# A third buffer for V, V's loads at other places, and a later opening behind each projection

## The chip, the cores and the metric

The kernel runs on one core of one Trainium2 chip. Its time is the device time of one execution in microseconds (us); the time of a version is the median of its runs. Five engines work side by side, each in the order of its own queue: TensorE (PE in the profile; its weight loads are PEld), VectorE (DVE), ScalarE (ACT), GpSimd (POOL) and SyncE (SP), which here only issues DMAs. Engines wait for each other, and for DMAs, through semaphores.

## The reference

Attention over normalised queries and keys, and behind it a feed-forward layer with x * cos(x):

```python
batch, n_heads, seq, head_dim = (8, 12, 448, 64)     # d_model 768, d_ff 2048, 3584 tokens
q_n = q / (norm(q) + 1e-06);  k_n = k / (norm(k) + 1e-06)
scores = q_n @ k_n.T / tau                            # tau = 0.1
attn = exp(scores - max(scores));  attn = attn / (sum(attn) + 1e-09)
x = (attn @ v) as [3584, 768]
h = x @ w_in;  g = h * cos(h);  out = g @ w_out
```

Inputs and output are float32. The kernel computes with bfloat16 operands and float32 sums.

## The kernel before

**Tiling.** The 96 heads are taken as 48 pairs of heads (g = 0 to 47). Three pairs make a unit (u = g // 3, 16 of them), two units a batch (6 pairs, 8 batches). Loads are made by unit, attention by pair, and the feed-forward layer by batch: the projection by w_in (`m1`) for all 448 tokens of a batch, the product with w_out (`m2`) in tiles of 128 tokens.

**A unit's way in.** SyncE loads the unit's k and q (`load`, raw). GpSimd squares them (sq, line 558), VectorE reduces the squares (n, line 565), ScalarE makes the reciprocal root by Ln and Exp (lnn and rn, lines 579 and 582), GpSimd multiplies (qks, line 590, labelled scale3.2 for unit 3, pair 2). A DMA transpose from SyncE's queue (line 607) puts the result into qkT; the first nine pairs are transposed on TensorE instead. V is loaded by `load_v` on GpSimd's DMA queue, two DMAs of 192 KB for a unit, into one of two buffers va (u % 2), so that the loads of a unit wait until the unit two before it has been used up.

**A pair.** `pair(g, f)` writes the scores of pair g (`scores(g, c)`, c = 0 to 3, on TensorE into the banks SC1, SC0, SC1, SC0, each followed by an Exp on ScalarE, line 652), and between them the product attn @ V of pair g - 1 (`attend`) and pieces of the output product (`m2_fill`, the four numbers in f, counted in steps of 0.16 us). `attend` has three stages. Stages 0 and 1 (R, line 669) open the accumulation of the values (with V) and of the sums of the exponentials (with ones) in the bank AV; they need one seventh of the keys (`exp` of c = 0). Stage 2 (lines 676 to 700) adds the rest.

**The way out of a pair.** For the pairs in `direct` (0 to 5 and 9 to 11), ScalarE makes the reciprocal of the sums by Ln and Exp (lines 728 and 730), and xT is made at once (line 736). For all others the unnormalised values and the sums are copied to xu (line 723), and once a unit `chain(u)` runs: four small DMAs on SyncE's queue gather the unit's sums (`gather`, line 745), VectorE adds and inverts them (rcp, lines 750 and 753), one DMA writes them to DRAM (`spread`, line 754), two bring them back spread over partitions (`bcast` into RB, line 756), and GpSimd multiplies (xT, line 760; labelled x17 for pair 17).

**Projections.** `m1(b)` is eight groups of 12 matmuls of 448 columns, over three bank pairs (AV, SC0, SC1). Behind each group ScalarE makes the cosine by Sin (line 789) and VectorE the product gT (line 791), which frees the bank. `m1` of batch 0 runs before pair 6, those of batches 1 to 6 behind the pairs 13, 21, 27, 33, 39 and 45 (`points`), with some steps of the output product behind them, and that of batch 7 at the end. The last group of a projection in `points` goes to AV, the one before it to SC1. ScalarE changes its table between Exp and Sin.

**Who sets the order.** TensorE's order is the order of the program, except in the prologue, where a window of 24 operations is open (and where matmuls on zeros fill its idle time). On the other four engines the order is made by a planner (`arrange` and `play`): it plays the program with costs, gives every operation a due time (`late`), and takes the ready one that is due first. DMAs are played as a flow with a time to take off (TAKEOFF), a time to land (LANDING), a share (`weight`) and a duration (`bulk`, the number behind the semaphore's name in each `dma` call); a transpose has an additional `lead`. `behind` (found by `find(label)`) puts an operation behind the issue of another one on the same engine. What comes out is a fixed queue for each engine.

## Time and profile before

| | |
|---|---|
| median of 3 runs | 442.57 us (442.4 to 443.27) |
| the profiled execution | 442.96 us |
| its span, first to last instruction | 441.2 us |
| granted TensorE clock | 0.998 |
| ScalarE, GpSimd, VectorE busy | 270.0, 227.9, 188.6 us |
| bytes moved by DMA | 64.80 MB, mean 147 GB/s |
| V: 32 DMAs of 192 KB, issue to landing, median | 8.8 us |
| k and q: 96 DMAs of 224 KB, median | 6.4 and 7.3 us |
| gathers of sums: 52 DMAs of 5.2 KB, median | 2.8 us |
| transposes: 39 DMAs, median | 4.5 us |

The page and the answers of the trace are read so. A row of a timeline has the start in us from the span's start, the time, the engine and line, the operation, and output<-input; in square brackets stands how long the engine was idle before it and what ended the wait. A row of the waits names who waited for whom, then the sum in us, the number of times and the longest. An idle engine costs nothing unless something that sets the end waits for it.

### The profile page before, as it was taken

Reading aid. Unit: us, or ns where it says so; the run is one execution under the profiler, and the core shown is the slowest. Engines: PE = TensorE matmul, PEld = TensorE weight load, DVE = VectorE, ACT = ScalarE, POOL = GpSimd, SP = SyncE. Lnnn points to the kernel's source line nnn. Section 1 sums busy time; section 2 is a strip of 40 time slices with the busy share of each in tenths; the row PEclk is TensorE's granted clock in tenths of the full one; section 3 lists DMA queues with packets and bytes.
Section 4 is the critical chain, followed back from the end, with each engine's and each line's share of the span. In section 5 each row is a group of like instructions: output and inputs, shape, how many; then the busy total and the mean of one; then the engine's idle time right before and its main releaser. Section 6 shows DMA issues by size and latency. Waiting matters only on the chain.

```text
span 441.2 us, 13512 instructions
## 1 busy us (share of the span) xinstructions
PE 419.4 (95%) x6049; PEld 231.2 (52%) x6049; DVE 188.6 (43%) x243; ACT 270.0 (61%) x352; POOL 227.9 (52%) x182
## 2 busy tenths in 40 slices
PE   7899979979998999999999999999999999999996
PEld 3344536635554645565556655565556645555563
DVE  3552852445833248330952158221952134223421
ACT  5886568685586755876487745786478745703400
POOL 4998909577390295916756095908656043002000
PEclk9999999999999999999999999999999999999999
DMA  8999999999358999649943997969966960151022
GB/s 193 248 252 218 250 184 144 180 193 201 78 85 141 173 206 198 114 109 212 242 106 74 175 218 157 129 133 217 213 100 90 140 139 3 39 138 36 1 71 71
DMA packets 80713, 64.80 MB, mean 147 GB/s; under 512 B 45712, under 2 KB 75408, under 8 KB 80656
## 3 DMA queue, kind: packets, MB, share of 16 engines
q1 hardware_dynamic: 62528, 51.16, 58.3%
q0 software_dynamic: 18048, 12.59, 19.0%
q8 instruction: 47, 0.77, 0.8%
q10 hardware_dynamic: 80, 0.20, 0.1%
q14 instruction: 10, 0.08, 0.1%
HBM read 56.13 MB, written 11.15 MB: 153 GB/s over the span
## 4 chain that ended last, share of the span: by engine, by line
PE 68%; DMA 10%; ACT 7%; issue 5%; POOL 4%; DVE 3%; SPq 2%; ACTq 0%; DVEq 0%; POOLq 0%
PE SC L774 18%; PE AV L774 10%; PE TP L849 9%; PE PO L849 8%; PE AV L676 5%; PE SC L637 5%; DMA sums<-xu 4%; ACT PX L652 3%; DMA va<-in_v_dram 2%; PE PO L879 2%; POOL xT L760 2%; PE AV L669 2%; POOL qks L590 2%; PE SC L879 2%; PE TP L879 2%
## 5 line engine op out<-in xcount | busy, mean ns | idle before, releaser
L652 ACT ACTIVATE PX<-SC 128x448 bf16<-128x448 f32 (+1 forms) x192 | 153.5, 824 | 33.7 <-PE SC L637 20.9
L849 PE MATMUL TP<-W,gT 64*64 64x384 bf16 x1408 | 143.7, 324 | 0.4
L849 PE MATMUL PO<-W,gT 64*64 64x384 bf16 x1408 | 143.7, 324 | 0.0
L590 POOL TENSOR_TENSOR qks<-raw,rn 128x896 bf16<-128x896 f32 (+1 forms) x48 | 79.2, 1675 | 45.3 <-ACT rn L582 43.5
L774 PE MATMUL SC<-xT,W 128*128 128x448 bf16 x480 | 98.6, 353 | 1.7 <-ACT PX L652 0.9
L760 POOL TENSOR_TENSOR xT<-xu,RB 128x448 bf16<-128x448 f32 x39 | 43.2, 1136 | 109.3 <-DMA RB<-scr 109.3
L849 PEld LDWEIGHTS PO<-W,gT 64*64 64x64 bf16 x1408 | 76.2, 107 | 17.7 <-DVE osb L822 3.0
L789 ACT ACTIVATE cosb<-SC,cst 128x896 f32<-128x896 f32 x40 | 40.2, 1007 | 72.8 <-PE SC L774 69.0
L849 PEld LDWEIGHTS TP<-W,gT 64*64 64x64 bf16 x1408 | 76.2, 107 | 16.2 <-PE TP L849 2.7
L558 POOL TENSOR_TENSOR sq<-raw 128x896 bf16<-128x896 f32 x45 | 74.9, 1683 | 8.3 <-DMA raw<-in_q_dram 5.0
L774 PEld LDWEIGHTS SC<-xT,W 128*128 128x128 bf16 x480 | 45.9, 98 | 47.0 <-POOL xT L760 2.9
L791 DVE TENSOR_TENSOR gT<-SC,cosb 128x896 bf16<-128x896 f32 x40 | 43.4, 1087 | 47.5 <-ACT cosb L789 47.3
L774 PE MATMUL AV<-xT,W 128*128 128x448 bf16 x288 | 61.8, 352 | 0.1
L565 DVE TENSOR_REDUCE n<-sq 128x14 f32<-128x896 bf16 (+2 forms) x49 | 51.4, 1054 | 10.0 <-ACT sq L556 6.0
L637 PE MATMUL SC<-qkT 64*64 64x448 bf16 x576 | 52.1, 359 | 3.4 <-ACT PX L652 3.0
L723 DVE COPY xu<-AV 128x896 f32<-128x896 f32 x25 | 27.1, 1085 | 46.4 <-PE AV L692 46.4
L822 DVE COPY osb<-PO 128x384 f32<-128x384 f32 x26 | 14.5, 557 | 71.5 <-PE PO L849 65.0
L774 PEld LDWEIGHTS AV<-xT,W 128*128 128x128 bf16 x288 | 28.1, 98 | 26.6 <-issue 0.5
L789 ACT ACTIVATE cosb<-AV,cst 128x896 f32<-128x896 f32 x24 | 24.1, 1005 | 21.3 <-PE AV L774 21.3
L676 PE MATMUL AV<-PX,va 128*32 128x448 bf16 x576 | 36.2, 356 | 0.0
L669 PE MATMUL AV<-PX,va 64*64 64x224 bf16 x192 | 25.6, 259 | 5.7 <-DVE gT L791 1.9
L791 DVE TENSOR_TENSOR gT<-AV,cosb 128x896 bf16<-128x896 f32 x24 | 26.1, 1087 | 9.9 <-ACT cosb L789 9.9
(60 smaller groups left out, 345.6 us busy)
## 6 DMA issues: line engine op xcount, KB each, us to landing
raw<-in_k_dram SPq DMA_DIRECT2D x48, 224.0 KB, 6.4
raw<-in_q_dram SPq DMA_DIRECT2D x48, 224.0 KB, 7.3
out_dram<-osb SPq DMA_DIRECT2D x55, 192.0 KB, 3.5
RB<-scr SPq DMA_DIRECT2D x26, 336.0 KB, 4.8
va<-in_v_dram POOLq DMA_DIRECT2D x32, 192.0 KB, 8.8
W<-in_moe_w_in_dram POOLq DMA_DIRECT2D x4, 768.0 KB, 15.1
W<-in_moe_w_out_dram POOLq DMA_DIRECT2D x4, 768.0 KB, 23.1
sums<-xu SPq DMA_DIRECT2D x52, 5.2 KB, 2.8
```

What stands on the lines that cost most here:

```text
L558: pool(lambda e, x=x, y=y: e.tensor_tensor(y, x, x, ALU.mult), src_, dst, 0.1 + n * 1.78e-3, label="sq%d.%d" % (u, p)).pad = LATE if u > 1 ...
L565: dve(lambda e, w=w: e.tensor_reduce(out=n2v[i][:, 2 * p : 2 * p + 2, w], in_=sqv[p][:, :, w, :], axis=mybir.AxisListType.X, op=ALU.add), ...
L590: f = lambda e, s0=s0, s1=s1: e.tensor_tensor(qksv[i][:, p, s0:s1].rearrange("p s h d -> p h s d"), rawv[i][:, h, s0:s1, :], bass.AP(rn[i] ...
L637: m = e.matmul(SCv[z][BP * o : BP * o + BP, a, 0:S], t[r, c - 1 + (NT3 + 1) * o, 0:BP], t[r, :, BP : 2 * BP], start=True, stop=True)
L652: act(lambda e: e.activation(PHv[j] if c == 0 else PXv[j][:, c - 1], SCv[z][:, :, 0:n], ACT.Exp, scale=1.0 / TAU), ["SC%d" % z], [("PX", j ...
L669: m = e.matmul(AVq[64 * a : 64 * a + 64, k, :, o, :], w, PHv[j][r, a, :], start=(n == 0), stop=False)
L676: t = e.matmul(AVv[o : o + 32, 0, 0:S], vav[i][:, 2 * p + a, c + 1, d : d + 32], PXv[j][:, c, a, :], start=False, stop=(c == NT3 - 1))
L760: pool(lambda e, p=p: e.tensor_tensor(xTv[b % 2][:, UP * i + p, :], xuv[:, u % 3, p, :], RBv[i][:, p, :], ALU.mult), [("RB", i, p), ("xa", ...
L774: t = e.matmul(ph[:, a, 0:S], W1v[:, c, 128 * n : 128 * n + 128], xTv[b % 2][:, c, :], start=(c == 0), stop=(c == NKC - 1))
L789: act(lambda e, ph=ph, cz=cz: e.activation(cosv[cz], ph[:, :, 0:S], ACT.Sin, bias=cst.ap()[:, 0:1], scale=1.0), names(gi) + ["cst0"], [("c ...
L791: dve(lambda e, ph=ph, cz=cz, gi=gi: e.tensor_tensor(gTv[:, 2 * gi : 2 * gi + 2, S * (b % 2) : S * (b % 2) + S], ph[:, :, 0:S], cosv[cz], ...
L849: r = e.matmul(POH[b][x : x + 64, 0:HW], gTv[k, y, col + x : col + x + 64], W2v[k, y, HW * b : HW * b + HW], start=(y == 0 and h == 0), st ...
```

## The change

It has four parts.

- **V's buffers and loads.** va has three buffers (u % 3). Inside `pair`, the load is for unit u + 2 where it was for u + 1, and starts at pair 9: V5 behind x8, V6 behind x11, V7 without `behind` but reading the sums buffer 0 (so it waits until the gather of unit 4 has landed), V8 behind x17 and so on. Ahead of that, V2 reads xT of pair 2, V3 stands behind the load W2.3, and V4, which was loaded inside pair 9, behind scale3.2.
- **The opening behind a projection.** In the pairs 14, 22, 28, 34, 40 and 46 (g - 1 in `points`), stage 0 of `attend` for the pair before is written behind `scores(g, 0)` and the first `m2_fill` instead of ahead of them. `points` moves up so that `pair` can see it.
- **The planner's numbers.** TAKEOFF, LANDING, the lead of a transpose, and the durations (and one weight) of transposes, gathers and bcasts.
- **iot.** The index tile of the prologue has no memory of its own; it lies in cosb0.

```diff
--- before.py
+++ after.py
@@ -39,8 +39,8 @@
     OVERLAP = {"ACT": 0.09, "DVE": 0.08, "POOL": 0.0, "SP": 0.0, "PE": 0.0}
     WINDOW = 24
     PATIENCE = 0.1
-    TAKEOFF = {"SP": 1.67, "ACT": 1.67, "POOL": 1.5}
-    LANDING = 0.6
+    TAKEOFF = {"SP": 1.85, "ACT": 1.85, "POOL": 1.6}
+    LANDING = 0.45
     BOTH = 1.09
     COLD = 2.7
     ROOM = 2200
@@ -410,7 +410,7 @@
     lnn = sbs("lnn", 2, [128, UH * NB], F32)
     rn = sbs("rn", 2, [128, UH * NB], F32)
     qks = sbs("qks", 2, [128, NB * UH * D], BF16)
-    va = sbs("va", 2, [128, UH * VS * D], BF16)
+    va = sbs("va", 3, [128, UH * VS * D], BF16)
     qkT = sbs("qkT", NT, [128, 2 * S], BF16)
     PX = sbs("PX", 2, [128, NB * S], BF16)
     xu = sb("xu", [128, 5 * UP * S], F32)
@@ -422,7 +422,7 @@
     ident = sb("ident", [128, 128], BF16)
     zt = sb("zt", [128, S], BF16)
     ones = sb("ones", [128, 96], BF16)
-    iot = sb("iot", [128, 128], I32)
+    iot = cosb[0].bitcast(I32).ap()[:, 0:128]
     cst = sb("cst", [128, 2], F32)
 
     SC = [ps("SC%d" % i, [128, 2 * 512], F32) for i in range(2)]
@@ -469,7 +469,7 @@
             if label.startswith(y):
                 took, descs = ISSUE[y]
         o = P.op(eng, lambda e: [f(e) for f in fns], reads, writes, cost=took * len(fns), dma=sem, bulk=bulk, label=label)
-        o.nd, o.descs, o.lead = len(fns), descs * len(fns), 0.75 if label[0] == "T" else 0.0
+        o.nd, o.descs, o.lead = len(fns), descs * len(fns), 0.3 if label[0] == "T" else 0.0
         o.weight, o.pad = weight, pad
         if behind is not None:
             P.order_only(behind, o)
@@ -502,8 +502,8 @@
     EXPSET = "natural_log_exp_and_others"
     SINSET = "trig_and_small"
 
-    pool(lambda e: e.iota(iot.ap(), [[1, 128]], base=0, channel_multiplier=-1), (), ["iot"], 0.25)
-    dve(lambda e: e.tensor_scalar(ident.ap(), iot.ap(), 0, None, ALU.is_equal), ["iot"], ["ident"], 128)
+    pool(lambda e: e.iota(iot, [[1, 128]], base=0, channel_multiplier=-1), (), [("cos", 0)], 0.25)
+    dve(lambda e: e.tensor_scalar(ident.ap(), iot, 0, None, ALU.is_equal), [("cos", 0)], ["ident"], 128)
     dve(lambda e: e.memset(cst.ap()[:, 0:1], math.pi / 2.0), (), ["cst0"], 1)
     dve(lambda e: e.memset(cst.ap()[:, 1:2], 1e-12), (), ["cst1"], 1)
     pool(lambda e: e.memset(ones.ap()[:, 0:64], 1.0), (), ["ones"], 0.15)
@@ -527,7 +527,9 @@
                 pad=LATE if u > 1 else 0.0)
 
     def load_v(u, behind=None, reads=()):
-        i = u % 2
+        if u >= NU:
+            return
+        i = u % 3
         b, hb = u // 2, UH * (u % 2)
         dma("POOL", [lambda e, z=z: e.dma_start(
             vav[i][BP * z : BP * z + BP, :, 1 - z : NT3 + 2 - z, :].rearrange("p h x d -> p h (x d)"),
@@ -606,7 +608,7 @@
         if g >= TD:
             dma("SP", [lambda e: e.dma_start_transpose(
                 qkTv[j], qks[i].ap()[:, NB * 2 * D * p : NB * 2 * D * (p + 1)])], [("qks", i, p, 0), ("qks", i, p, 1)],
-                [("qkT", j, 0), ("qkT", j, 1)], "T%d" % j, 1.17, "T%d" % g, None, 10.0)
+                [("qkT", j, 0), ("qkT", j, 1)], "T%d" % j, 1.4, "T%d" % g, None, 10.0)
             return
 
         def half(e, bank, s0, s1):
@@ -656,7 +658,7 @@
 
     def attend(g, direct, stages=(0, 1, 2)):
         u, p, j = g // UP, g % UP, g % 2
-        i, b = u % 2, g // PB
+        i, y, b = u % 2, u % 3, g // PB
         AVq = AVv[:, :, 0:S].rearrange("p x (s o m) -> p x s o m", s=NB, o=2)
         ws = slice(0, 64) if direct else slice(32, 96)
 
@@ -665,7 +667,7 @@
                 o = n ^ k
                 r = slice(BP * o, BP * o + BP)
                 for a in range(2):
-                    w = vav[i][r, 2 * p + a, 0 if o else VS - 1, :] if k == 0 else ones.ap()[r, ws]
+                    w = vav[y][r, 2 * p + a, 0 if o else VS - 1, :] if k == 0 else ones.ap()[r, ws]
                     m = e.matmul(AVq[64 * a : 64 * a + 64, k, :, o, :], w, PHv[j][r, a, :],
                                  start=(n == 0), stop=False)
             return m
@@ -673,7 +675,7 @@
         def av(e, c):
             for o in range(0, 128, 32):
                 a, d = o // 64, o % 64
-                t = e.matmul(AVv[o : o + 32, 0, 0:S], vav[i][:, 2 * p + a, c + 1, d : d + 32], PXv[j][:, c, a, :],
+                t = e.matmul(AVv[o : o + 32, 0, 0:S], vav[y][:, 2 * p + a, c + 1, d : d + 32], PXv[j][:, c, a, :],
                              start=False, stop=(c == NT3 - 1))
             return t
 
@@ -701,7 +703,7 @@
 
         for n in stages:
             if n < 2:
-                o = P.op("PE", lambda e, n=n: rest(e, n), [("va", i), ("PX", j, 0), "ones", "zeros"], ["AVa", "AVs"],
+                o = P.op("PE", lambda e, n=n: rest(e, n), [("va", y), ("PX", j, 0), "ones", "zeros"], ["AVa", "AVs"],
                          cost=HALF, mode="Q", label="R%d" % g)
                 if n:
                     P.settled(opened[g], o)
@@ -709,7 +711,7 @@
         if 2 not in stages:
             return
         for c in range(NT3):
-            P.op("PE", lambda e, c=c: av(e, c), [("va", i), ("PX", j, c + 1)], ["AVa"], cost=MM + (0.021 if c == 0 else 0),
+            P.op("PE", lambda e, c=c: av(e, c), [("va", y), ("PX", j, c + 1)], ["AVa"], cost=MM + (0.021 if c == 0 else 0),
                  mode="C32", label="AV%d" % g)
         if not direct:
             P.op("PE", sm, ["ones", ("PX", j, 1), ("PX", j, 2)], ["AVs"], cost=MM, mode="C32", label="S%d" % g)
@@ -745,7 +747,7 @@
         dma("SP", [lambda e, r=r, a=a: e.dma_start(
             sums[i].ap()[64 * a : 64 * a + 64, SPR * r : SPR * r + SPR],
             bass.AP(xu, ((64 * a + 32 * r) * 5 + 3 + i) * UP * S, [[5 * UP * S, 1], [SPR, 64], [1, SPR]]))
-            for r in range(2) for a in range(2)], [("xs", i, p) for p in range(UP)], [("sums", i)], "sums%d" % i, 0.4,
+            for r in range(2) for a in range(2)], [("xs", i, p) for p in range(UP)], [("sums", i)], "sums%d" % i, 0.7,
             "gather%d" % u)
         dve(lambda e: e.tensor_reduce(out=rcp[i].ap(), in_=sums[i].ap().rearrange("p (r x) -> p x r", r=2),
                                       axis=mybir.AxisListType.X, op=ALU.add), [("sums", i)], [("rcp", i)], 2 * SPR,
@@ -755,7 +757,7 @@
             [("rcp", i)], [("scr", u)], "scr", 0.02, "spread%d" % u)
         dma("SP", [lambda e, a=a: e.dma_start(
             RBv[i][64 * a : 64 * a + 64], bass.AP(scr, (u * 2 + a) * UP * S, [[0, 64], [1, UP * S]])) for a in range(2)],
-            [("scr", u)], [("RB", i, p) for p in range(UP)], "RB%d" % i, 3.2, "bcast%d" % u, None, 1.0, 0.5)
+            [("scr", u)], [("RB", i, p) for p in range(UP)], "RB%d" % i, 3.4, "bcast%d" % u, None, 2.4, 0.5)
         for p in range(UP):
             pool(lambda e, p=p: e.tensor_tensor(xTv[b % 2][:, UP * i + p, :], xuv[:, u % 3, p, :], RBv[i][:, p, :], ALU.mult),
                  [("RB", i, p), ("xa", u % 3, p)], [("xT", b % 2, UP * i + p)], 1.1, label="x%d" % (UP * u + p))
@@ -947,6 +949,8 @@
         a = min(y for y in [step * x for x in range(cycle)] + [2 * NF] if y >= at) - at
         return (a + 1) // 2, a // 2, c, d
 
+    points = {PB * (b + 1) + (1 if b == 1 else 3): b for b in range(1, B - 1)}
+
     def pair(g, f):
         u, p = g // UP, g % UP
         if 3 <= u < NU - 1:
@@ -956,10 +960,12 @@
                 norms(u + 1, 1)
         late = g > PB
         quarters = g >= PB
-        if late:
+        if late and g - 1 not in points:
             attend(g - 1, direct(g - 1), (0,))
         scores(g, 0)
         m2_fill(f[0], quarters)
+        if late and g - 1 in points:
+            attend(g - 1, direct(g - 1), (0,))
         scores(g, 1)
         if late and f[1] and quarters:
             attend(g - 1, direct(g - 1), (1,))
@@ -975,8 +981,9 @@
                     chain(u - 1)
                 if g > PB and (u <= 3 or u % 2 == 0):
                     loads(u + 2, find("bcast%d" % (2 if u == 4 else u - 1)) if u > 3 else None)
-                if u + 1 < NU and u != 1:
-                    load_v(u + 1, find("x%d" % (g - 1 if u % 2 == 0 else g - 4)) if u > 4 else None)
+                if g > PB:
+                    load_v(u + 2, None if u == 5 else find("x%d" % (g - 1 if u < 5 or u % 2 == 0 else g - 4)),
+                           [("sums", 0)] if u == 5 else [])
         if g == PB:
             m2_fill(f[1], True)
         if g + 2 < PB:
@@ -1008,7 +1015,7 @@
     load_w1(3, find("scale1.0"))
     for x in range(NQ):
         load_w2(x, find("scale1.1"))
-    load_v(2)
+    load_v(2, None, [("xT", 0, 2)])
     norms(2, 0)
     norms(2, 1)
     loads(3)
@@ -1017,12 +1024,12 @@
     for g in range(PB, TD):
         transposes(g)
     m1(0, 2, NKC - 1)
-    load_v(3)
+    load_v(3, find("W2.3"))
     norms(3, 1)
+    load_v(4, find("scale3.2"))
     loads(4)
     P.free = False
     m2_add(0)
-    points = {PB * (b + 1) + (1 if b == 1 else 3): b for b in range(1, B - 1)}
     for g in range(PB, NG):
         pair(g, (0, 5, 0, 6) if g == PB else shares(3 if 2 * PB + 1 < g <= 3 * PB + 1 or g >= NG - 2 else 2))
         if g in points:
```

## The prediction

> **What bounds the kernel now.** I read the engine line of the page first, then TensorE's waits by stretch, then the timelines of VectorE, ScalarE, SyncE and GpSimd around the two stretches with the longest waits.
>
> The page says how far a gain can go:
>
> ```profile
> PE 419.4 (95%) x6049; PEld 231.2 (52%) x6049; DVE 188.6 (43%) x243; ACT 270.0 (61%) x352; POOL 227.9 (52%) x182
> ```
>
> TensorE is busy for 419.4 of the 441.2 us of the span. It works in the order written, so the end moves only by what its 21.8 us of idle time gain or lose: 5.7 in the first 44 us, 2.6 at 62 us (behind the first projection), 4.3 in the tail after its last matmul, and waits between. TensorE's waits, first from 85 to 100 us and then from 101 us to the end:
>
> ```profile
> PE SC L645 <- ACT PX L652: 1.2, 2, 0.6
> PE AV L669 <- ACT xu L728: 1.0, 1, 1.0
> PE SC L774 <- ACT PX L652: 0.9, 1, 0.9
> PE SC L637 <- ACT PX L652: 0.4, 1, 0.4
> PE AV L669 <- issue: 0.2, 1, 0.2
> ```
>
> ```profile
> PE AV L669 <- DVE gT L791: 1.9, 4, 0.5
> PE AV L669 <- DVE xu L723: 1.2, 1, 1.2
> PE SC L774 <- POOL xT L760: 0.8, 4, 0.3
> PE PO L879 <- DVE osb L822: 0.7, 1, 0.7
> ```
>
> The first list sums to 3.7 us, all of it ended by ScalarE. Why ScalarE is late stands in the timelines of SyncE, GpSimd, VectorE and ScalarE from 77 to 91 us:
>
> ```profile
> 79.11 3.33 SPq L745 DMA_DIRECT2D sums<-xu  x4
> 82.54 1.25 SPq L607 DMA_TRANSPOSE qkT<-qks  x1
> ```
>
> ```profile
> 77.97 1.35 POOL L532 DMA_DIRECT2D va<-in_v_dram  x2 [1.08 <-PE AV L692]
> ```
>
> ```profile
> 87.28 0.20 DVE L750 TENSOR_REDUCE rcp<-sums 128x21 f32<-128x42 f32 x1 [4.15 <-DMA sums<-xu]
> 87.72 2.02 DVE L565 TENSOR_REDUCE n<-sq 128x14 f32<-128x896 bf16 x2
> 89.66 0.61 DVE L735 COPY xu<-AV 128x448 f32<-128x448 f32 x1
> ```
>
> ```profile
> 89.77 0.33 ACT L579 ACTIVATE lnn<-n,cst 128x42 f32<-128x42 f32 x1 [2.87 <-DVE n L565]
> 90.28 0.53 ACT L728 ACTIVATE xu<-AV 128x448 f32<-128x448 f32 x1
> ```
>
> V of unit 4 is issued at 77.97, the gather of the sums of unit 2 right behind it at 79.11. The gather's four pieces land 5.4 to 7.5 us after issue (the reads and writes of the sums in that window). VectorE stands 4.15 us at rcp; behind it in its queue are two reductions n and the copy of pair 9; ScalarE stands 2.87 us at lnn, which wants those n, and behind lnn is the Ln of pair 9 (line 728) that frees TensorE's bank. From 90.28 ScalarE works almost without a break until 100.3, so its 2.87 us are lost to the end. The same thing happens at 126 us with V of unit 6 (issued 126.02), in VectorE's timeline:
>
> ```profile
> 135.22 0.20 DVE L750 TENSOR_REDUCE rcp<-sums 128x21 f32<-128x42 f32 x1 [4.31 <-DMA sums<-xu]
> 135.66 1.03 DVE L723 COPY xu<-AV 128x896 f32<-128x896 f32 x1
> ```
>
> Here the copy that frees TensorE's bank is behind rcp, and TensorE loses 1.2 us. A gather with no V beside it (237 to 243 us) takes this from issue to landing:
>
> ```profile
> DMA to landing us min/median/max: 2.0/2.1/2.2
> ```
>
> **(a) The gather of unit 2.** With three buffers V4 no longer waits for pair 8's matmuls (the 1.08 us before 77.97). It is free behind scale 3.2, which is the third of the six products that GpSimd runs from 65.34 in 9.92 us, so from some 70.3. By the planner's due times I put it at about 72, behind scale 4.0. Two things follow. The two squares behind V4 in the old order end 1.08 us sooner, the wait that V4 had, so one or both n can run before rcp; and the gather no longer has 384 KB starting just ahead of it. At best the 2.87 us of ScalarE's idle time go (TensorE's 3.7 are not all to be had: the bank waits behind 90.28 are ScalarE's own 10 us of work). At worst nothing: V4's bytes then precede the raw loads of 70 to 79 us, the DMA engines are as full there, and the whole queue ahead of the gather is late by as much. Between 0 and 2.87 I take 2.3: the end nearer to the undisturbed 2.1 us, but not all of it, as a transpose is issued at 82.54 right behind the gather, as one was at 130.96 in the second case.
>
> [...]
>
> **(b) The gather of unit 4.** V6 goes from 126.02 to behind x11, before the projection of batch 1, and V7 comes only after this gather has landed (it reads the sums). Without V6 ahead, the transpose issued at 127.06, which took 5.0 us to land, has 2.6 like the one issued at 123.10, and the last piece (issued 130.26, landed 135.20) has the 2.0 of one issued at 142.03, which also had a transpose 0.7 us behind it. Rcp then runs at some 132.5, the copy waits for its matmuls alone. Between 0 and 1.2 I take 1.0. V7 has GpSimd wait for the gather; queued behind it are only the products of unit 4, which wait for RB until 143.3 anyway.
>
> **(c) Opening later.** Four of the six pairs behind a projection have R (line 669) wait for the last gT: 0.46 us at 119.9, 224.6 and 323.5, 0.53 at 274.2. Now SC.0 goes first; its bank SC1 was freed one group (2.27 us) sooner. At 323.94 in TensorE's timeline R runs, then SC.0 at 324.03, three steps of the output product from 324.13 to 324.61, then SC.1. Put ahead of R, SC.0 and the three steps take 0.1 + 0.48 = 0.58 us, more than the 0.46 or 0.53. For the pairs 28, 34 and 40 the wait is gone: 0.46 + 0.53 + 0.46 = 1.45. Pair 14 has the other share (no steps between SC.0 and SC.1), so only SC.0's 0.1 moves into its wait. Pairs 22 and 46 had no wait and neither gain nor lose. Sum 1.55; if gT came later still (it is VectorE's, with n queued between), 1.0. I take 1.5.
>
> **(d) What costs nothing.** V from unit 8 on is issued at the same release as now (x17, x23 and so on), for a unit later, so with its due time later it goes behind the squares. The gathers beside projections (160 to 309 us, 6.9 to 9.2 us) may land sooner, but TensorE lost nothing to them: their results are wanted some 30 us later. If that cover were gone it would show as TensorE waiting for xT, 0.8 us in all now. V15 leaves the last projection (356.52), where nothing waits for it. The 128 columns of iot go into cosb0, first written at 46.8 us, long after ident was made of them at 1.1.
>
> **(e) The planner's new constants** change no instruction, only the order on ScalarE, VectorE, GpSimd and SyncE. TAKEOFF plus LANDING changes from 2.27 to 2.30 on SyncE and from 2.10 to 2.05 on GpSimd; a transpose is reckoned 0.2 cheaper in all, a gather 0.3 dearer. No row prices a new order. Bounds: the best is that the waits for xT and osb go too (0.8 + 0.7 = 1.5 gained), the worst that transposes come as much later (1.5 lost; the nearest of them lands 2.2 us before its scores, issued 326.37, landed 331.09, wanted 333.26). I take 0, in the middle.
>
> **The sum.** 2.3 + 1.0 + 1.5 = 4.8 us. The profiled run took 442.96 (its span 441.2 and 1.8 around it), so 438.2 for it; the median of the runs is 0.39 lower, so 437.8, with the span at 436.4. Its own range, by (a) from 1.2 to 2.87 and (e) at about half its bounds, is 436.3 to 439.3.
>
> **Rivals.**
> *The move of V4 gains nothing* because the DMA engines are full from 70 to 80 us, but (b) and (c) hold: 442.57 - 2.5 = 440.1. For it: the raw loads issued at 73.4 and 74.1 need 5.1 and 5.4 us, against 3.3 for the first load of all. Against: the n can run sooner whatever the gather does.
> *The gathers are held by the transposes*, not by V: (a) and (b) are gone, 442.57 - 1.5 = 441.1. For it: at 130 us V6 had landed at 131.1, yet the gather's last two pieces landed at 134.9 and 135.2, beside the transpose's 135.6. Against: pieces with a transpose 0.7 us behind them (142.03, 338.64) landed in 2.0 and 2.6 us.
> *Slower: V's bytes hold up the raw loads, and lnn stands at ScalarE's head.* V5 and V6 now both go out behind x8 and x11, between 96 and 101 us, where raw loads already need 5 to 7 us and GpSimd's squares wait for them (2.21, 0.34 and 0.24 us at 109 to 113). If V6 makes these loads late by its own 4.0 us (issued 126.02, first half landed 130.04), the n are late by as much, lnn, now at 120.39, blocks the exponentials of pair 14, and ScalarE's idle time costs TensorE 3.7 / 2.87 = 1.28 of itself as at 90 us: 5.1 us. V4 does the same to the squares of unit 5, and (a) is gone. 442.57 - 2.5 + 5.1 = 445.2. It decides from some 2 us of lateness on: squares end at 115, and the last n runs at 120.1 behind gT, so there are 2 to 5 us of cover, which speaks against it.
> *It does not do what it says*: the planner puts V4 and V7 beside gathers again and an order elsewhere loses what (c) gains: 442.5.
>
> **How the numbers follow.** The forecast has 0.53, V4 for nothing 0.12, transposes 0.12, slower 0.11, no effect 0.05, and 0.07 is for a gain above 6.3 (a, b and c at their best and part of (e)), below 436.3. The time is 437.8. The range goes from 435.4 (most of that last case) to 441.3, so that both partial rivals are in it and the slower one and no effect are out. A change below 0.2% (0.9 us) can't be told from none here. Faster by more: 0.53 + 0.12 + 0.12 + 0.07 = 0.84, of which 0.01 goes to the middle for a partial gain that shrinks; within it 0.06; slower 0.11.
>
> **What would show it.** For (a): V4 issued near 72, no idle time of some 3 us ahead of lnn near 90, and TensorE's waits for ScalarE from 85 to 100 at 1.5 us or less. For (b): no V between 120 and 130, rcp near 132 and no 1.2 us wait for xu. For (c): the four waits of AV L669 for gT down to one of 0.4. For (e): waits for xT and osb as they are. Wrong it is if TensorE waits for a transpose or for V, or if lnn or a product on GpSimd stands longer for raw loads than now.

## The result, and the profile after

The changed kernel is slower: 447.5 us, the median of 10 runs (443.73 to 449.01), against 441.99 us for before in the same comparison (440.73 to 443.27). The ratio is 1.0116, with a 95% interval of 1.0083 to 1.0149; a second comparison of the same two kernels (run e11 below) gave 1.0066 (1.0034 to 1.0098). Forecast were 437.8 us and a ratio of 0.989. The profiled execution took 448.73 us, its span 445.9, at a granted clock of 0.990.

The page's engine line, of after:

```profile
PE 424.0 (95%) x6054; PEld 233.2 (52%) x6054; DVE 189.2 (42%) x243; ACT 269.4 (60%) x352; POOL 227.9 (51%) x182
```

TensorE is idle for as long as before (445.9 - 424.0 = 21.9 us, before 21.8), but busy 4.6 us longer, with the same work. So waits have moved from one place to another, and the same matmuls take longer. TensorE's waits in after, from 60 to 101 us and from 101 us to the end:

```profile
PE SC L639 <- ACT PX L654: 3.0, 2, 2.6
PE TP L851 <- issue: 2.1, 1, 2.1
PE SC L647 <- ACT PX L654: 0.6, 1, 0.6
PE AV L671 <- issue: 0.2, 1, 0.2
```

```profile
PE SC L776 <- POOL xT L762: 2.9, 8, 1.1
PE SC L776 <- ACT PX L654: 1.6, 1, 1.6
PE PO L881 <- DVE osb L824: 0.7, 1, 0.7
PE AV L671 <- DVE gT L793: 0.4, 1, 0.4
PE AV L671 <- DVE xu L725: 0.3, 1, 0.3
```

What was to go has gone: of four waits of R for gT one is left, the 1.2 us for xu has become 0.3, and no wait near 90 us is for the Ln of pair 9. What has come: 2.1 us ended by "issue", which is no wait for any engine or DMA that the profile shows; and the projections' waits for xT, 2.9 us in place of 0.8. The new stall, in TensorE's timeline:

```profile
79.67 0.32 PE L851 MATMUL TP<-W,gT 64*64 64x384 bf16 x1
79.67 0.32 PE L851 MATMUL PO<-W,gT 64*64 64x384 bf16 x1
82.06 0.47 PE L851 MATMUL TP<-W,gT 64*64 64x384 bf16 x1 [2.06 <-issue]
82.06 0.52 PE L851 MATMUL PO<-W,gT 64*64 64x384 bf16 x1
```

It stands amid a run of equal matmuls of the output product, whose operands had long been there; and behind it the same matmul takes 0.52 us in place of 0.32. Busy time by stretch, of after, with the granted clock (the first number behind the five engines) and the share of the DMA engines:

```profile
64.00:68.40 4.40, 3.50 (x48) 2.21 (x52) 0.00 (x0) 3.23 (x7) 2.98 (x2) 0.61 0.32 45
79.00:82.00 3.00, 0.99 (x24) 0.36 (x13) 2.08 (x2) 1.02 (x2) 1.12 (x1) 1.00 1.25 221
82.00:85.50 3.50, 3.44 (x44) 2.47 (x47) 0.00 (x0) 0.92 (x1) 1.68 (x1) 0.51 1.09 180
```

The clock is 0.61 behind the wait of 2.6 us at 62 us, and 0.51 behind the new stall. In the trace each is a stretch of 3.41 us at half clock, which costs some 1.7 us of matmul time. In before's profiled execution the clock is 1.00 in all three stretches, though its wait at 62 us was as long.

Pairs start later or earlier than before as follows (scores of pair g, after minus before): pair 7 +1.45 (half clock), pair 10 +5.45 (stall and half clock), pair 12 +3.53 (the stall at 90 us is gone), pair 18 +2.70 (the gather of unit 4), pair 22 +4.63 (second projection), pairs 29, 35 and 41 +4.31, +4.08 and +3.57 (the openings), end +4.7.

What stood in SyncE's, GpSimd's, VectorE's and ScalarE's timelines around the first gather, in after:

```profile
72.09 1.33 SPq L609 DMA_TRANSPOSE qkT<-qks  x1
...
80.69 2.44 SPq L747 DMA_DIRECT2D sums<-xu  x4
83.96 1.23 SPq L609 DMA_TRANSPOSE qkT<-qks  x1
```

```profile
72.16 1.35 POOL L534 DMA_DIRECT2D va<-in_v_dram  x2
...
83.70 1.68 POOL L560 TENSOR_TENSOR sq<-raw 128x896 bf16<-128x896 f32 x1 [3.58 <-DMA raw<-in_q_dram]
```

```profile
89.51 0.19 DVE L752 TENSOR_REDUCE rcp<-sums 128x21 f32<-128x42 f32 x1
```

```profile
92.27 0.32 ACT L581 ACTIVATE lnn<-n,cst 128x42 f32<-128x42 f32 x1
```

V4 went out at 72.16 as reckoned, and neither rcp nor lnn has a wait in front of it. But the gather still took 5.0 to 6.1 us to land (80.69 to 87.50), the transpose issued at 72.09 took 10.0 us (that of the same pair in before 5.4), and GpSimd's square stood 3.58 us for raw loads. The DMA engines are that full: the packets that start from 70 to 79 us take 1.15 times the 16 engines' time of that stretch (1.02 in before). The trace shows one more user of them: queue q8, kind "instruction", with 47 packets and 0.77 MB in all, 16 KB each. TensorE has 6054 matmuls and as many weight loads; 0.77 MB over 12,108 is 64 bytes for each, so this is taken for TensorE's own program being fetched; that is an estimate, as the trace doesn't say for which engine the queue works. In before's first trace these blocks start at 68.10, 73.71, 79.70 and 84.07 us. In after they start at 67.57 and 77.94, and the second takes 2.46 us in place of 0.9 to 1.7.

### The profile page after: what moved, and what is told of

It is laid out like the page before. It is cut to its first block, busy times and chain, and to the rows that moved or that the text cites. A ratio compares the mean times of both kernels' runs of the same rounds, so it can differ in the third digit from the quotient of the medians.

```text
span 445.9 us, 13527 instructions
## 1 busy us (share of the span) xinstructions
PE 424.0 (95%) x6054; PEld 233.2 (52%) x6054; DVE 189.2 (42%) x243; ACT 269.4 (60%) x352; POOL 227.9 (51%) x182
## 4 chain that ended last, share of the span: by engine, by line
PE 65%; issue 9%; POOL 8%; DMA 7%; ACT 6%; DVE 2%; SPq 1%; POOLq 0%; ACTq 0%; DVEq 0%
PE SC L776 19%; PE AV L776 10%; PE TP L851 9%; PE PO L851 8%; PE AV L678 5%; PE SC L639 4%; POOL xT L762 3%; POOL qks L592 3%; ACT PX L654 3%; DMA scr<-rcp 2%; DMA RB<-scr 2%; PE AV L671 2%; PE SC L881 1%; PE TP L881 1%; PE PO L881 1%
## 5 line engine op out<-in xcount | busy, mean ns | idle before, releaser
L851 PE MATMUL TP<-W,gT 64*64 64x384 bf16 x1408 | 146.3, 328 | 2.5 <-issue 2.1
L851 PE MATMUL PO<-W,gT 64*64 64x384 bf16 x1408 | 146.1, 328 | 0.0
L851 PEld LDWEIGHTS PO<-W,gT 64*64 64x64 bf16 x1408 | 77.1, 108 | 20.8 <-issue 4.9
L851 PEld LDWEIGHTS TP<-W,gT 64*64 64x64 bf16 x1408 | 77.7, 108 | 16.5 <-PE TP L851 2.7
L639 PEld LDWEIGHTS SC<-qkT 64*64 64x64 bf16 x576 | 16.3, 106 | 23.5 <-ACT PX L654 12.5
```

Of the source, the lines that this page charges most:

```text
L639: m = e.matmul(SCv[z][BP * o : BP * o + BP, a, 0:S], t[r, c - 1 + (NT3 + 1) * o, 0:BP], t[r, :, BP : 2 * BP], start=True, stop=True)
L851: r = e.matmul(POH[b][x : x + 64, 0:HW], gTv[k, y, col + x : col + x + 64], W2v[k, y, HW * b : HW * b + HW], start=(y == 0 and h == 0), st ...
```

## The experiments

In four groups; within a group all kernels and before share a chip. Every one has five rounds against before (12 runs, e9 6).

**The parts, each alone.** e1 has only the later opening, e2 only the planner's numbers, e3 only the third buffer and V's places, and e4 is the changed kernel with V4 behind the last load of w_out (about 47 us) in place of scale3.2 (72 us):

```diff
# e4, against the changed kernel
-    load_v(4, find("scale3.2"))
+    load_v(4, find("W2.3"))
```

> The kernel before with the later opening alone. Theory (V4's bytes at 72 us hold up TensorE's instruction fetch, and the idle time halves its clock): the opening is no part of the loss; 1.0 to 1.5 us faster than before, the three gT waits of 0.5 us gone, no wait ended by issue near 80 us. Rival (the opening costs): slower than before by 1 us or more.

> The kernel before with the planner's new constants alone. Theory: within 1 us of before, no wait of TensorE ended by issue near 80 us. Rival (the planner's new order is what loses): 3 to 5 us slower.

> Third buffer and V's new places alone, with the constants and the opening of before. Theory: 4 to 6 us slower than before, as the whole change is; the transpose issued near 72 us needs about 10 us to land, TensorE waits some 2 us for issue near 80 and has half its clock in the window behind it. Rival (planner's order): within 1 us of before.

> The changed kernel with V4 right behind V3 (at some 48 us) instead of behind scale3.2 (72 us). Theory: V4 has landed by 71, the transposes of 72 and 76 us land within 6 us, the wait for issue near 80 us (2.1) and the half clock behind it (1.7 us lost) are gone: 3.8 us faster than the changed kernel, some 443.5. Rival: as slow as the changed kernel, 447.5.

Measured: e1 0.9994 (0.9966 to 1.0022), e2 0.9995 (0.9968 to 1.0021), e3 1.0084 (1.005 to 1.0118), e4 1.0034 (1.0001 to 1.0068). The loss comes with V's places: e3 alone has 0.0084, where the whole change has 0.0116 and, in e11 below, 0.0066. In e4's trace V4 lands at 66 to 68 us, the instruction blocks come at 67.22, 73.16 and 79.38, there is no stall, the transpose takes 5.1 us, and the gather of unit 2 lands in 2.0 to 2.8 us. In e1's trace the waits for gT are gone (1.66 us by the starts of the pairs), but its time doesn't show it: where 1.0 to 1.5 us were expected, the medians are 0.2 us apart, and the interval admits 1.5 us at most. e3 loses a little less than its theory's 4 to 6 us, with a stall of 0.36 us where some 2 were expected, and no half clock behind it. Both e1 and e2 leave V4 where before has it, and in their traces only 2.0 us are left of the waits that sum to 3.7 us around 90 us: the clock was halved at 65 us and the gather landed in 2.6 to 3.8 us. That wait, on which the forecast's largest term rests, is tested again with e16.

**V7, and the wait at 62 us.** e5 has V7 behind x17 in place of the gather, e6 the edits of e4 and e5, e7 is e6 with 7 matmuls on zeros written into the wait of 2.6 us, e8 the changed kernel with these. Their result is not used.

```diff
# e5, e6, e7
+                    if u == 6:
+                        load_v(7, find("x%d" % (g - 1)))
+                    if u != 5:
+                        load_v(u + 2, find("x%d" % (g - 1 if u < 5 or u % 2 == 0 else g - 4)))
-                    load_v(u + 2, None if u == 5 else find("x%d" % (g - 1 if u < 5 or u % 2 == 0 else g - 4)),
-                           [("sums", 0)] if u == 5 else [])
# e7, e8
         if g == PB:
             m2_fill(f[1], True)
+            P.op("PE", lambda e: [e.matmul(AVv[:, 0, 0:S], zt.ap()[:, 0:128], zt.ap(), start=True, stop=True)
+                                for _ in range(7)][-1], ["zt"], ["AVa", "AVs"], cost=7 * MM, mode="F", label="fill")
```

> The changed kernel with V7 behind x17 (at some 158 us) instead of behind the gather of unit 4 (136 us). Theory: V7's bytes beside the broadcast of unit 4 and the gather of unit 5 make the second projection wait 1 to 2.4 us for xT; without them that wait falls to 0.3 or less and the kernel is 2 us faster than the changed one, some 1.007 of before. Rival (V4 is all of the loss): as slow as the changed kernel, 1.011.

> V4 early (as in the run before) and V7 behind x17. Theory: both losses gone and the gains of opening later and of the free gathers of units 2 and 4 kept: 0.995 of before (2 us faster), TensorE idle for 4 us less than in the changed kernel. Rival (the gains were an accident of one trace): 1.000 to 1.003.

> The kernel with V4 early and V7 late, and seven matmuls of zeros (into the bank that is free there) in the 2.6 us for which TensorE waits behind the first projection; their result is not used. Theory (a wait of over 2 us costs another 1.7 us, since the granted clock halves for 3.4 us when the wait fills enough of a window of that length): no half clock at 65 us, 1 us faster than without them. Rival (the half clock there is made up for later, as ScalarE is behind anyway): no difference.

> The changed kernel with the same seven matmuls of zeros behind the first projection. Theory: one of its two windows of half clock goes, the one behind the wait for issue at 80 us stays: 1 to 1.7 us faster than the changed kernel, 1.008 of before. Rival (the clock is made up for later): 1.011.

Measured: e5 1.0060 (1.0025 to 1.0096), e6 1.0008 (0.9969 to 1.0046), e7 1.0003 (0.997 to 1.0036), e8 1.0056 (1.0027 to 1.0084). V7's place is not what has the second projection (the one behind pair 21) wait for xT: e5 has that wait still, 1.63 us, so its theory fails. e6 has 1.0008 where 0.995 was expected; e12 below shows part of the reason. The filled wait has no half clock behind it in the traces of e7 and e8, yet e7 is no faster than e6, and e8 is still slow: the half clock at 65 us is not the loss, or not alone. e5 to e6, V4's place alone, is 0.0052.

**V4 alone.** e9 is before with the third buffer and V4 at 72 us, every other V at its old place in the program; e10 the same with V4 at 47 us. With the third buffer, loads at their old places no longer wait for a buffer: V5 goes out at 82.6 us in e9 and 82.8 in e10 (before 94.8), V6 at 111.7 and 107.8 (before 126.0). e11 is the changed kernel once more. e12 is e6 with the planner's old numbers.

```diff
# e9 (e10: find("W2.3")), against before
+    load_v(4, find("scale3.2"))
-                if u + 1 < NU and u != 1:
+                if u + 1 < NU and u not in (1, 3):
# e12, against e6
-    TAKEOFF = {"SP": 1.85, "ACT": 1.85, "POOL": 1.6}
-    LANDING = 0.45
+    TAKEOFF = {"SP": 1.67, "ACT": 1.67, "POOL": 1.5}
+    LANDING = 0.6
...
```

> Only V of unit 4 is moved (third buffer, behind scale3.2, so about 72 us); every other load of V, the planner's numbers and the opening are those of before. Theory 'V4 at 72': its 384 KB, the raw loads and the transposes fill the DMA engines from 72 to 80 us, the block of instructions due at about 73 comes only at 77 or later, and TensorE stands 0.3 to 2.1 us near 80 us (with some half-clock time behind it): ratio 1.005 to 1.010, like the kernel with all of V moved (1.0084). Rival 'the order of spreads and transposes and V5 to V7': V4 alone costs nothing, ratio 0.998 to 1.002, or 0.995 as the prediction had it.

> The same with V4 behind the last load of w_out (about 47 us) in place of 72. Theory 'V4 at 72': the blocks of instructions come every 5 to 6 us, no stall near 80 us, the gather of unit 2 lands in 2.0 to 2.8 us, and the stall of 3.7 us at 90 us stays away: ratio 0.995 to 1.000, at least 0.006 below the kernel with V4 at 72. Rival: no difference between the two, both within 0.998 to 1.002.

> The changed kernel itself, on the same chip as the three others. Both theories: ratio 1.008 to 1.015 as in its first comparison. A trace of another execution of it: by 'V4 at 72' the block of instructions due at 73 us is again 4 us late or more, and the stall near 80 us is between 0 and 2.1 us.

> The changed kernel with V4 at 47 us, V7 behind x17, and the planner's old numbers; against the same with the new numbers (ratio 1.0008 to its before) SyncE's queue differs in the order of the spreads and the transposes: the spread of units 2, 4, 6 and 8 goes ahead of the transpose beside it again. Theory 'the order takes back what V4 and the opening gain': the spread lands within 2 us of issue, the wait for xT at the second projection falls from 0.9 to 1.6 us to 0.4 or less, and the ratio to 0.992 to 0.997. Rival 'the order doesn't matter': ratio 0.998 to 1.003, xT waits as before.

Measured: e9 1.0102 (1.0068 to 1.0136), e10 1.0035 (1.0015 to 1.0056), e11 1.0066 (1.0034 to 1.0098), e12 0.9971 (0.9944 to 0.9999). Between e9 and e10 are 0.0067, or 3.0 us, for one load's place, as the theory had it. Both are slower than they should be by something else: the planner sent V0 at 1.39 us in both, ahead of raw loads (before at 5.57), and in e10's trace pair 6 starts 3.3 us late. So e10 missed its number (0.995 to 1.000), and this pair speaks for the difference only.

e11 missed two of the three things expected of it: the ratio is below 1.008 to 1.015, and the block expected 4 us late came in time; the stall, 0.15 us, is within the 0 to 2.1 named. Its trace is another execution of the same program, with a span of 440.6 us, 5.3 us shorter, and it shows what the 5.3 us are. Waits from 60 to 101 us, then the stretches:

```profile
PE SC L639 <- ACT PX L654: 3.0, 2, 2.6
PE SC L776 <- POOL xT L762: 1.9, 1, 1.9
PE SC L647 <- ACT PX L654: 0.6, 1, 0.6
```

```profile
64.00:68.40 4.40, 3.42 (x80) 2.04 (x84) 0.00 (x0) 4.32 (x8) 2.92 (x2) 1.00 0.19 27
...
79.00:82.00 3.00, 3.00 (x83) 1.93 (x76) 1.50 (x3) 2.53 (x4) 1.02 (x1) 1.00 1.15 295
82.00:85.50 3.50, 3.35 (x78) 2.10 (x74) 2.27 (x4) 2.33 (x4) 1.68 (x1) 1.00 1.25 167
```

The wait of 1.9 us for xT, at the projection behind pair 13, is another matter and comes back under e12. Near 80 us there is no wait for issue but one of 0.15 us at 84 us, too short to show in the list, and the clock is 1.00 in all three. 2.06 for the stall and twice 1.7 for the half clock make 5.5 us; by the starts of the pairs the two executions part by 1.3 us at pair 7, by 3.9 at pair 10, and by little else. The DMA queues from 69 to 77 us, first of e11, then of after (queue, packets, MB, share of the 16 engines):

```profile
q1 hardware_dynamic: 1585, 1.17, 89.2%
q0 software_dynamic: 219, 0.11, 17.7%
q8 instruction: 1, 0.02, 1.0%
```

```profile
q1 hardware_dynamic: 1344, 1.11, 72.6%
q0 software_dynamic: 367, 0.18, 23.9%
```

In e11 a block of instructions got through at 73.53; in after none did until 77.94, beside more of V's packets (q0). V4 went out within 0.1 us of the same time in both. So with V4 at 72 us the block can come in time or late, from one execution to the next: the two traces show both. The spread of the runs shows less: the 22 of the changed kernel lie from 442.34 to 450.89 us, but the 29 of before in e11's comparison also lie as far apart as 439.16 to 445.10.

e12 came out at the edge of its theory's range (0.9971, where 0.992 to 0.997 was expected). In SyncE's queue it differs from e6 at the spreads of three units, 2, 7 and 11: with the new numbers a transpose stands ahead of each, with the old ones behind it, and two outputs move with those of 7 and 11. Around the spread of unit 2, first e6, then e12, with the first matmuls of the projection behind pair 13:

```profile
85.12 3.05 SPq L826 DMA_DIRECT2D out_dram<-osb  x2
88.21 1.34 SPq L609 DMA_TRANSPOSE qkT<-qks  x1
89.60 0.58 SPq L756 DMA_DIRECT2D scr<-rcp  x1
93.04 1.12 SPq L758 DMA_DIRECT2D RB<-scr  x2
...
101.97 1.45 PE L776 MATMUL SC<-xT,W 128*128 128x448 bf16 x4 [3.89 <-POOL xT L762]
```

```profile
84.39 2.35 SPq L826 DMA_DIRECT2D out_dram<-osb  x2
86.79 0.59 SPq L756 DMA_DIRECT2D scr<-rcp  x1
87.43 1.23 SPq L609 DMA_TRANSPOSE qkT<-qks  x1
89.20 1.12 SPq L758 DMA_DIRECT2D RB<-scr  x2
...
98.82 1.29 PE L776 MATMUL SC<-xT,W 128*128 128x448 bf16 x6 [0.94 <-POOL xT L762]
```

In e6 the spread is issued 2.81 us later, 1.38 of it for the transpose ahead and 1.43 for the output DMAs that end later, and it takes 3.42 us to land in place of 2.39. GpSimd's products of unit 2 start at 98.53 in place of 95.35, the projection stands 3.89 us for them in place of 0.94, and TensorE's clock is halved behind that, at 102.2 us: pair 14 starts 4.63 us later by it. This execution of e6 is its longest run (447.89 us). But the wait stands in six of the seven traces with the new numbers and V's new places, 1.4 to 3.9 us long (in after, the seventh, TensorE waits 1.6 us for ScalarE there), and with the old numbers and V4 moved it is 0 to 1.2 us in seven traces.

At the second projection e12 has no wait for xT over 0.2 us, while the longest in after is 1.1. There the order is not the reason: around the spread of unit 4 it is the same in all versions, a transpose 2.6 to 4.8 us ahead of the spread and the next one 0.5 to 1.2 us behind it. This spread lands in 1.6 to 1.8 us in the four traces with V6 where before has it, and in the fourteen others in 2.6 to 2.8 (e10, e12 to e15) or in 4.4 to 6.6. V7 beside it isn't needed for the late ones (e5, e6, e7 and e9 have V7 over 20 us later, and 4.4 to 5.0), nor are the new numbers (e3 and e9 have the old ones). What holds it up there stays open.

Waits of e12 from 101 us on:

```profile
PE SC L776 <- POOL xT L762: 1.3, 6, 0.5
PE PO L881 <- DVE osb L824: 0.7, 1, 0.7
PE AV L671 <- DVE gT L793: 0.4, 1, 0.4
```

**The shares.** e13 is e12 with V4 back at 72 us, e14 e12 with the opening of before, e15 e12 with the 7 matmuls on zeros of e7, e16 the kernel before.

```diff
# e13, against e12
-    load_v(4, find("W2.3"))
+    load_v(4, find("scale3.2"))
# e14, against e12
-        if late and g - 1 not in points:
+        if late:
...
-        if late and g - 1 in points:
-            attend(g - 1, direct(g - 1), (0,))
```

> The version with the planner's old numbers (V4 at 47 us, V7 behind x17, ratio 0.9971), and in it V4 alone put back to 72 us, behind scale3.2; the prologue on TensorE and its whole order are the same in both. Theory 'V4 at 72 us costs some 3 us, by the block of instructions that comes late and by TensorE's clock behind the stall': ratio 1.002 to 1.008, and single runs spread over 6 us or more. Rival 'the move of V4 is free, the loss is in the planner's new numbers': 0.995 to 0.999.

> The same version (V4 at 47 us, old numbers) with the opening of before. Theory 'the opening is worth the 1.5 us that the waits for gT in the trace say': ratio 1.000 to 1.002. Rival 'the opening gives its gain back elsewhere': 0.996 to 0.998, no different from the version with it.

> The same version with 7 matmuls on zeros in the wait of 2.6 us behind the first projection (their result is not used). Theory 'the half-clock stretches behind that wait cost 1 to 1.5 us in most executions': ratio 0.992 to 0.995. Rival 'they come as often elsewhere': 0.996 to 0.998.

> The kernel before, unchanged: a second trace of it. Theory 'the stall of 3.7 us at 90 us belongs to single executions': TensorE's waits for ScalarE from 85 to 100 us are below 2.6 us here if the clock was halved behind the wait at 62 us, and 3 us or more if not. Rival 'it is in every execution': 3.3 to 4.1 us in any case. Ratio 0.998 to 1.002 by both.

Measured: e13 1.0034 (1.001 to 1.0059), e14 0.9991 (0.9961 to 1.0022), e15 0.9985 (0.9958 to 1.0011), e16 0.9995 (0.9977 to 1.0014). V4's place by itself, with TensorE's whole order the same, is 0.0063 between e12 and e13, and the intervals don't meet (the two are of different groups). e13's profiled execution happened to be its shortest run (438.45 us). Its block came at 72.88, the next one at 81.92, and the stall is there all the same, small:

```profile
84.55 0.35 PE L851 MATMUL PO<-W,gT 64*64 64x384 bf16 x1 [0.77 <-issue]
```

The same stall, for issue and between equal matmuls of the output product, stands in all seven traces with V4 at 72 us, between 80 and 88 us: 2.06 (after), 0.77 (e13), 0.48 (e9), 0.42 (e5), 0.36 (e3), 0.15 (e11), 0.14 us (e8). None of the other eleven has one there. Each of the seven ends 1.45 to 1.79 us after the packet of an instruction block has ended.

Which block is late goes with the clock at 65 us. With the half clock there, the block behind the one near 68 us (70 in e1, e9 and e10) comes 9.05 to 10.4 us after it in the four traces with V4 at 72 us (after, e3, e5, e9), and 6.8 to 8.6 in the seven with V4 elsewhere. Without it that block is in time, and the next one comes 7.9 to 9.0 us after it in the three with V4 at 72 us (e8, e11, e13), and 6.0 to 6.5 in the four with V4 elsewhere. The ranges are apart in both cases. But a distance of 8 us alone makes no stall: e12 has 8.6 and none.

e15 says that filling the wait at 62 us gains nothing that can be measured, for the second time (0.992 to 0.995 was expected). e14 lies 0.0020 above e12, where the opening's waits are 1.5 us or 0.0034; the intervals overlap, so the opening's worth stays open. e16's waits from 85 to 100 us:

```profile
PE SC L645 <- ACT PX L652: 1.1, 2, 0.6
PE SC L774 <- ACT PX L652: 0.9, 1, 0.9
PE SC L637 <- ACT PX L652: 0.4, 1, 0.4
PE AV L669 <- issue: 0.2, 1, 0.2
```

The wait for xu is not there. The list sums to 2.6 us where the first trace had 3.7 (each with 0.2 ended by "issue"). In this execution of before the clock was halved at 65 us (pair 7 starts 1.18 us later than in the first trace) and 1.26 us of it came back at pair 12. Whichever came, pair 12 starts at 91.75 and 91.77 us. The wait at 90 us is slack that takes up the delay at 65.

**The sum by steps.** From before to after, each row one edit more:

| version | ratio to before | step |
|---|---|---|
| e12: later opening, third buffer, V4 at 47 us, V7 behind x17, old numbers | 0.9971 | -0.0029 |
| e13: V4 at 72 us | 1.0034 | +0.0063 |
| e5: the planner's new numbers | 1.0060 | +0.0026 |
| after: V7 behind the gather | 1.0116 and 1.0066 | +0.0056 and +0.0006 |

V4's step is shown three times (e12 to e13, e10 to e9, e6 to e5: 0.0063, 0.0067, 0.0052), with intervals apart in the first two. A fourth pair, e4 to after, has 0.0082 by after's first comparison and 0.0032 by its second. What it consists of is located in part: the seven stalls have a mean of 0.63 us, and the mean granted clock is 0.9942 over the 76 runs with V4 at 72 us against 0.9960 over the 84 with V4 at 47, which over 442 us would be 0.8. That these 0.8 us are V4's isn't shown: between e12 and e13, which differ in V4's place alone, the clock is 0.9952 and 0.9951. So 1.7 to 2.4 us of the 2.3 to 3.0 remain that the profiled executions don't place, or 0.9 to 1.6 with the clock counted. The gather, which lands some 3 us later, is one candidate, and that is argued only. The new numbers are +0.0026 here and +0.0037 from e12 to e6; all four intervals are too wide for one such step to be settled, and so are those of V7.

## Why the prediction was wrong, step by step

**(a), the gather of unit 2, 2.3 us gained: this step failed, twice.** Its mechanism fits the traces: behind V4's bytes the gather lands later. With V4 at 47 us it lands in 2.0 to 3.5 us in all seven traces (2.0 to 2.4 in e12); with V4 at 72 us in 2.8 to 6.3 in seven (5.0 to 6.1 in after). But the bound "at worst nothing" was false. The step saw that the DMA engines are full from 70 to 79 us (1.02 times their time in before) and asked only who of the known waiters would be late. It didn't ask who else draws on these engines. By the estimate above TensorE does, for its own instructions (47 blocks of 16 KB), and with 95% of the span busy it has the least room to be late. Against a place at 47 us, this place cost 0.0052 to 0.0067, or 2.3 to 3.0 us, where a gain of 0 to 2.87 against the old place (78 us) stood; no version has that move of 6 us and nothing else. The stall is the part of the cost that the traces show best, 2.06 us in the profiled execution. And the price was read off one execution: the 3.7 us at 90 us (3.5 for ScalarE; the row ended by "issue" was counted in) were 2.6 in the second trace, and what was missing there had been lost at 65 us. A wait behind which an earlier delay vanishes is worth nothing when it is removed, as long as the delay is there.

**(b), the gather of unit 4, 1.0 us gained: right, then in part taken back.** Its pieces land in 2.0 us as said, and pair 18 gains 1.38 us against pair 17. Here too the price was of one execution: the wait of 1.2 us for xu is 0.7 in before's second trace (e16). What the step left out is the spread behind the gather: it takes 2.6 to 6.6 us in the fourteen traces with V6 out of the way and 1.6 to 1.8 in the four with V6 in its old place, and in after (4.6 us) the second projection then waits 1.06 us for xT. V7, which the step put there and of which it said that only products are queued behind it, isn't needed for that (e5 has V7 elsewhere, a spread of 4.8 us and a wait of 1.63).

**(c), the opening, 1.5 us gained: as forecast in the trace**, where the waits at the pairs 28, 34 and 40 are gone (in e1, which has only the opening, 0.51, 0.64 and 0.51 by the starts of the pairs, together 1.66 us) and the one of 0.4 at pair 14 is left. In the times it can't be told: e1 0.9994, e12 against e14 -0.0020.

**(d), nothing: not tested by itself.** The sign named for it, TensorE waiting for xT, came: of the 2.9 us in after, 1.38 are at the second projection and 1.17 at the one behind pair 45, where before has 0.16 and 0.66. e12, with all of these later loads, has neither (0.16 and 0), so they don't make these waits alone.

**(e), the planner's numbers, 0 in a range of 1.5 either way: the mechanism was missed.** Alone they do nothing (e2 0.9995). With V's new places they put a transpose ahead of the spread of unit 2 (with before's places, in e2, they don't), and the projection behind pair 13 waits for xT, 3.89 us in e6 against 0.94 in e12. The steps from e13 to e5 and from e12 to e6 point to 0.0026 and 0.0037, 1.1 to 1.6 us, at the loss end of the range, but their intervals overlap. The step looked at transposes coming late. What came late was the small DMA behind one.

**The rivals.** The slower one had the right part of the kernel, V's bytes against what is loaded beside them, and 445.2 us, nearest to the result; but its place and its price were others. Lnn has no wait in front of it at 92.27 us, and while squares wait for raw loads (3.58 us), TensorE doesn't wait for them. "V4's move gains nothing" and "the gathers are held by the transposes" ended on the wrong side. Of the signs by which the prediction called itself wrong, one came: a product on GpSimd, the square at 83.70 us, stood 3.58 us for raw loads, where the longest such wait in before is 2.21. TensorE waiting for a transpose or for V didn't come: in both lists of waits above no row has them. The wait that came on TensorE is one for which the profile names nobody. One reading in the prediction is off and changes nothing above: (a) and (e) as stated give its own range as some 436.5 to 439.7 us, not 436.3 to 439.3.

The best version is e12: 441.11 us, ratio 0.9971 (0.9944 to 0.9999), some 1.3 us ahead of before, little more than can be told. In its trace pairs 18 to 21 start 2.2 us earlier than in before's first trace and pair 40 2.6 us (1.8 and 2.7 us against e16's), without the stall and with a wait of 0.94 us at the projection behind pair 13.

## What to carry to other kernels

Before a transfer is moved into a stretch where the DMA engines are full (1.02 times their time here), list everything that uses them there, with the program of the busiest engine among it: a wait ended by "issue" in the middle of equal instructions (2.06 us in after), and a gap in the instruction queue (10.4 us), were its signs here. A stall that stands in one profiled execution is priced only once a second one shows it, and a delay ahead of it is looked for that it may be taking up. And a small DMA in a chain went out as late as what stood ahead of it in its queue (the spread of unit 2 in e6 2.81 us later than in e12, 1.38 of it for a transpose), so the order around such chains is to be looked at by itself.

## What the runs showed of the hardware

The blocks of queue q8, taken for TensorE's instructions, came later with V4 beside them: blocks that come every 4.4 to 6.0 us in before's first trace (68.10 to 84.07 us) were 10.4 us apart in after, where at the same clock the versions with V4 elsewhere have at most 8.6, and TensorE stood 2.06 us until 1.66 us after the late block was in. A stall of this kind, 0.14 to 2.06 us, stands in seven traces of seven with V4's 384 KB in that stretch and in none of the eleven others. That the late block is the cause is read from the order of events and the distances of the blocks; no run delayed a block by itself.

TensorE's clock was halved in after for 3.41 us behind waits of 2.60 us (at 62 us) and 2.06 us (at 80 us). The same program does so in one execution and not in another: before is at 1.00 in its first trace and at a half from 64.64 to 68.05 us in e16's. In the traces it goes with where the wait falls. Counted in steps of 3.41 us from a change of the clock, from 20 to 420 us in all 18 traces, each of the 15 steps in which TensorE, at full clock, stood for 2.03 us or more has half clock behind it, and no step with 1.86 us or less has. In before's first trace the wait at 62 us falls into two such steps (1.57 and 1.03 us idle), in e16's into one (2.60). Why the clock does so, the traces don't show.
